# Other PSUM banks for the down projection, and the last two output products in halves of 160 columns

## The chip, the cores and the metric

The kernel runs on one core of a Trainium2 chip. The metric is the device time of one execution in microseconds; the median of three runs of the kernel before is 878.79 us (878.28 to 879.32). Beside the timed runs there is one profiled execution, from which all durations of instructions come.

## The reference, cut to what matters

```python
xn = layernorm(x)                                   # x: 2048 rows of 640, bf16
s  = attention(xn, k_cache, v_cache, wq, wo)         # 32 heads of 192, the last 512 keys
h  = silu(xn @ w_gate) * (xn @ w_up)                 # 2048 x 1536
g  = silu(h @ w_down)                                # 2048 x 640, the "down projection"
out = x + s * g                                      # s ends in the product with wo: 6144 -> 640
```

The change touches two products: `h @ w_down` and the last product with `wo`.

## The kernel before, in words

The kernel has three stages, one after the other on TensorE: the feed-forward part (to about 167 us), the attention (to about 690 us) and the output projection with the final multiply and add (to the end). The order of the work is written out by hand: each engine executes its instructions in the order in which the kernel emits them, and semaphore waits are put in by the framework from what each instruction reads and writes. For the PSUM tiles of the down projection these waits go by whole tile: an instruction that writes one half of a tile of two banks waits for an earlier reader of the other half.

**The feed-forward part.** Rows go in four blocks of 512 (`b` = 0 to 3). For each block twelve steps make gate and up products of 128 hidden columns (`ffn_hidden`, line 394: ten matmuls of 512 columns). Beside the steps of block `b` runs the down projection of block `b - 1`, so for the last block it runs alone, at the end of the stage (146 to 167 us). It is done by Strassen's scheme in Winograd's form, with seven products instead of eight for a 2 x 2 split: `ffn_down(b, u)` (line 442) takes a *row pair*, 128 rows and the 128 rows that stand 256 further on, `u` = 0 or 1, so two row pairs a block. It returns seven steps, which the caller issues in the order `w1, w2, w6, w5_, w7, w3, w4`, and `rest`. Each step is a product of six matmuls with 320 columns (line 456), and then reads by other engines:

- `w1`: product into bank U; ScalarE copies U to `p1` (line 478); for all but one row pair the sums S1 and S2 on VectorE follow here, for the first row pair of the last block they are made earlier (line 515).
- `w2`: product into bank V; VectorE makes `p1` = V + `p1` (line 484, in the helper at line 462).
- `w6`: adds a product with S2 to U; ScalarE copies U to `u2` (line 488) and applies the gate to `p1`; VectorE makes S3.
- `w5_`: product into bank W; ScalarE copies W to `w5` (line 494); VectorE makes S4.
- `w7`: adds a product with S3 to U; VectorE makes `w5` = U + `w5`.
- `w3`: adds a product with S4 to W; VectorE makes `u2` = W + `u2`; ScalarE gates `w5`.
- `w4`: adds a product to U; ScalarE gates U; the result is stored on SP's queue.

The banks are four halves of two PSUM tiles, `down_banks[0:4]`: 0 and 1 are the two banks of the first tile, 2 and 3 of the second. The kernel before takes three in rotation, from `3 * (2 * b + u)` on, modulo 4:

```
row pair        before (U, V, W)        tiles of U, V, W
b even, u = 0   0, 1, 2                 1st, 1st, 2nd
b even, u = 1   3, 0, 1                 2nd, 1st, 1st
b odd,  u = 0   2, 3, 0                 2nd, 2nd, 1st
b odd,  u = 1   1, 2, 3                 1st, 2nd, 2nd
```

For block 3, the last, the steps are issued one after the other; between them stand only products of the attention's first queries (`q_full`, line 523, five matmuls of 512 columns): for `u` = 0 one ahead of `w1`, one after `w5_` and one after `w4`; for `u` = 1 one after `w2`, one after `w5_` and one after `w4`. VectorE also makes combinations of `xc` (line 543) after `w2`, `w5_` and `w3`.

**The output projection.** Eight pairs of row tiles (`n` = 0 to 7), each again by seven products `M1, M7, M2, M5, M6, M4, M3` (`run`, `product`, line 942: 24 matmuls of 320 columns each, each with its own weight load). Each of the accumulators is a PSUM bank of its own, from a pool of eight. M3 adds to the bank that M5 began. After the last product, M3 of `n` = 7, the kernel has already multiplied and added all else (`u`), so two VectorE operations of 320 columns remain (line 979 in the helper `total`: the product times g, plus `u`), then the store of these 320 columns on ScalarE's queue.

Of the kernel before, what the change touches and what calls it, by code (L numbers as in the profile page):

```python
# [10 lines left out]
ALU = mybir.AluOpType  # L11
# [4 lines left out]
def kernel(  # L16
# [13 lines left out]
    nc = tc.nc  # L30
# [9 lines left out]
    W = min(4096, max(256, Sk // 4))  # L40
# [11 lines left out]
    HC = D // 2  # L52
# [27 lines left out]
    def sc_tile():  # L80
        return sc_pool.tile([P, 2, 512], f32, name="sc")

    def mm_tile(which=None):
        which = mm_next[0] if which is None else which
        mm_next[0] = 1 - which
        return mm_pool[0].tile([P, 2, 512], f32, name="mm", tag="mm%d" % which)
# [12 lines left out]
    M1, M7, M2, M5, M6, M4, M3 = PRODUCTS = range(10, 17)  # L99
# [127 lines left out]
    a_q, b_w = {}, {}  # L227

    with ExitStack() as fctx:
# [45 lines left out]
        for t in range(4, 8):  # L275
# [9 lines left out]
        first = [  # L285
            [gu[:, s, :] for s in range(2)]
            for gu in (sc_tile(), sc_tile(), psum1.tile([P, 2, 512], f32, name="gu"))
        ]
# [143 lines left out]
        down_banks = []  # L432
# [9 lines left out]
        def ffn_down(b, u):  # L442

            if not down_banks:
                down_banks.extend(t[:, n, 0:HC] for t in (mm_tile(), mm_tile()) for n in range(2))
            at = 3 * (2 * b + u)
            U, V, W = (down_banks[(at + k) % 4] for k in range(3))
            g = {}

            def a(side, k):  # L450
                rows = slice((u + 2 * side) * P, (u + 2 * side + 1) * P)
                return hTs[b][:, k * KD : (k + 1) * KD, rows]

            def mm(m, left, ps, first=True):
                for c in range(KD):
                    nc.tensor.matmul(  # L456
                        ps, left[:, c, :], D_OF[m][:, c, :],
                        start=(first and c == 0), stop=(c == KD - 1), skip_group_check=True,
                    )

            def total(to, x, y, op=ALU.add):
                nc.vector.tensor_tensor(to, x, y, op)

            def gate(side, n, x):
                nc.scalar.activation(g[side][:, n * HC : (n + 1) * HC], x, ACT.Silu)

            def store(side):
                nc.sync.dma_start(out=g_d[4 * b + u + 2 * side, :, :], in_=g[side][:])

            def sums():  # L470
                total(S1, a(1, 0), a(1, 1))
                total(S2, S1, a(0, 0), ALU.subtract)

            def w1():
                for side in range(2):
                    g[side] = ffa.tile([P, D], bf, name="g_t", bufs=2)
                mm(W1, a(0, 0), U)
                nc.scalar.copy(p1, U)
                if (b, u) != (NB - 1, 0):
                    sums()  # L480

            def w2():
                mm(W2, a(0, 1), V)
                total(p1, V, p1)

            def w6():
                mm(W6, S2, U, False)
                nc.scalar.copy(u2, U)
                gate(0, 0, p1)
                total(S3, a(0, 0), a(1, 0), ALU.subtract)  # L490

            def w5_():
                mm(W5, S1, W)
                nc.scalar.copy(w5, W)
                total(S4, a(0, 1), S2, ALU.subtract)

            def w7():
                mm(W7, S3, U, False)
                total(w5, U, w5)

            def w3():
                mm(W3, S4, W, False)
                total(u2, W, u2)
                gate(1, 1, w5)

            def w4():
                mm(W4, a(1, 1), U, False)
                gate(1, 0, U)
                store(1)

            def rest():
                gate(0, 1, u2)
                store(0)

            if (b, u) == (NB - 1, 0):
                sums()
            return [w1, w2, w6, w5_, w7, w3, w4], rest
# [93 lines left out]
        for b in range(NB):  # L611
# [3 lines left out]
            for f in range(NF):  # L615
# [15 lines left out]
                at = (b - 1) * NF + f  # L631
# [302 lines left out]

        nc.vector.tensor_tensor(a_s[n, m][:], part(x), part(y), op)

    def product(n, m, ps, first=True, ns=1):
        at = a_s[n, m] if (n, m) in a_s else a_q[n, A_OF[m][0]]
        w = HC // ns
        for k in range(ns):  # L940
            for c in range(KH):
                nc.tensor.matmul(  # L942
                    ps[k] if ns > 1 else ps, at[:, c, :], b_w[m][:, c, k * w : (k + 1) * w],
                    start=(first and c == 0), stop=(c == KH - 1), skip_group_check=True,
                )

    def load_xg(n):
        for side, r in enumerate(ROW_PAIRS[n]):
            tag, bufs = ("khat", 2) if n % 2 == 0 else (("K_p", "KT")[side], 1)
            t = xg[n, side] = kpool.tile([P, 2, D], bf, name="xg", tag=tag, bufs=bufs)  # L950
            nc.sync.dma_start(out=t[:, 0, :], in_=x2[r * P : (r + 1) * P, :])
            nc.sync.dma_start(out=t[:, 1, :], in_=g_d[r, :, :])
# [3 lines left out]
    def f_tile(n, k):  # L956
        return temps[:, 4 * (n % 2) + k, :]

    def finish(n, side, k, s, in_psum=False):

        t, cols = xg[n, side], slice(k * HC, (k + 1) * HC)
        y = f_tile(n, 3) if in_psum else s
        nc.vector.tensor_tensor(y, s, t[:, 1, cols], ALU.mult)
        nc.vector.tensor_tensor(t[:, 0, cols], y, t[:, 0, cols], ALU.add)

    def store(n, side, cols=slice(0, D), eng=nc.sync):
        r = ROW_PAIRS[n][side]
        eng.dma_start(out=out2[r * P : (r + 1) * P, cols], in_=xg[n, side][:, 0, cols])

    V = nc.vector  # L970

    ORDER = [(n, m) for ms in ((M1, M7), (M2,), (M5,), (M6,), (M4,), (M3,)) for n in range(2) for m in ms]
# [3 lines left out]
    acc = {}  # L976

    def total(to, x, y, op=ALU.add):
        V.tensor_tensor(to, x, y, op)

    def bank(n, name):
        acc[n, name] = late[1].tile([P, 512], f32, name="acc")[:, 0:HC]
        return acc[n, name]

    def run(n, m):

        ahead = n + 2 < len(ROW_PAIRS)
        u, v, c = (f_tile(n, k) for k in range(3))
        if m == M1:
            ps = bank(n, "M1+M2")  # L990
            product(n, M1, ps)
            nc.scalar.copy(u, ps)  # L992
        elif m == M7:
            ps = bank(n, "M7+M4")
            product(n, M7, ps)
            nc.scalar.copy(v, ps)
        elif m == M2:
            ps = acc[n, "M1+M2"]
            product(n, M2, ps, first=False)
            finish(n, 0, 0, ps, in_psum=True)  # L1000
            if (n, M3) == ORDER[-1]:
                store(n, 0, slice(0, HC))
        elif m == M5:
            ps = bank(n, "M5+M3")
            product(n, M5, ps)
            total(v, ps, v)
        elif m == M6:
            ps = bank(n, "M6")
            product(n, M6, ps)
            total(u, ps, u)  # L1010
            total(v, u, v)
            finish(n, 1, 1, v)
            for q in (A11, A21) if ahead else ():
                load_a(n + 2, q)
        elif m == M4:
            ps = acc[n, "M7+M4"]
            product(n, M4, ps, first=False)
            total(c, ps, u)
            finish(n, 1, 0, c)
            store(n, 1)  # L1020
            if ahead:
                load_a(n + 2, A22)
        else:
            ps, t, last_cols = acc[n, "M5+M3"], xg[n, 0], slice(HC, D)
            if (n, m) == ORDER[-1]:
                total(u, u, t[:, 1, last_cols], ALU.mult)
                total(u, u, t[:, 0, last_cols])
            product(n, M3, ps, first=False)
            if (n, m) == ORDER[-1]:
                total(c, ps, t[:, 1, last_cols], ALU.mult)  # L1030
                total(t[:, 0, last_cols], c, u)
                store(n, 0, last_cols, nc.scalar)
            else:
                total(u, ps, u)
                finish(n, 0, 1, u)
                store(n, 0)
            if ahead:
                load_a(n + 2, A12)
                load_xg(n + 2)
        if (n, m) in A_SUMS:  # L1040
            k = A_SUMS.index((n, m)) + 3
            if k < len(A_SUMS):
                a_sum(*A_SUMS[k])
# [46 lines left out]
    for n in range(4):  # L1090
        part = (n * KH // 4, (n + 1) * KH // 4)
# [80 lines left out]
    for n, m in ORDER:  # L1172
        run(n, m)
# [30 lines left out]
```

## Time and profile before

| | us |
|---|---|
| median of three runs | 878.79 |
| profiled execution | 878.91 |
| its span, first to last instruction | 877.1 |
| TensorE busy | 867.6 |
| VectorE busy | 603.5 |
| ScalarE busy | 427.5 |
| GpSimd busy | 114.2 |

The mean granted TensorE clock is 1.000. The 1.8 us between the span and the time of the profiled execution lie outside what the profile shows. In lines of the trace in order of time, the first number is the start in us from the span's start, the second the length of the group in us, then engine, line, operation, output and inputs, shapes and count; in brackets stands how long the engine had been idle just before, and what ended that. "PE" is TensorE's matmuls, "PEld" its weight loads, "SPq" and "ACTq" are the instructions that issue transfers. A matmul's duration (0.299 us for 320 columns) is longer than the distance to the next one's start (0.136 us), since matmuls are pipelined.

### The profile page before, as it was taken

The page shows a single profiled execution, that of the slowest core. Times are in us where ns is not written, and L with a number is a line of the kernel's source. Part 1 is how long each engine was busy: PE and PEld are TensorE (multiplying, and loading weights), DVE is VectorE, ACT ScalarE, POOL GpSimd, SP SyncE. Part 2 cuts the span into 40 slices and gives each one's busy share as a digit, 9 for nine tenths or more (in the row PEclk, how much of TensorE's full clock was granted, in tenths as well). Part 3 has the DMA queues.
Part 4 walks back from the last instruction along what each step waited for, and adds up shares of the span by engine and source line. Part 5 has one row for each costly group of instructions (what it writes and reads, how often), then busy time and mean ns, then how long its engine had stood idle before and what let it go on. Part 6 is the DMA issues. An engine that isn't in the chain of part 4 may idle for free.

```text
span 877.1 us, 22922 instructions
## 1 busy us (share of the span) xinstructions
PE 867.6 (99%) x9641; PEld 576.2 (66%) x9657; DVE 603.5 (69%) x1028; ACT 427.5 (49%) x649; POOL 114.2 (13%) x217
## 2 busy tenths in 40 slices
PE   8999999999999999999999999999999999999998
PEld 5455555567667667667667667667667777777775
DVE  6765876676876876876876876877775556555553
ACT  4264433665765765765765765765767300000000
POOL 0000000112122122122122132132120000000000
PEclk9999999999999999999999999999999999999999
DMA  9669974258999988977987777978899998645510
GB/s 294 172 210 275 214 222 116 67 98 180 204 204 217 201 179 200 195 162 176 198 177 179 176 149 163 208 165 189 167 230 251 255 355 294 212 171 176 176 54 16
DMA packets 273432, 165.52 MB, mean 189 GB/s; under 512 B 174384, under 2 KB 268208, under 8 KB 272816
## 3 DMA queue, kind: packets, MB, share of 16 engines
q1 hardware_dynamic: 271824, 156.08, 73.8%
q10 hardware_dynamic: 1504, 7.96, 2.6%
q8 instruction: 76, 1.25, 0.6%
q14 instruction: 28, 0.23, 0.1%
HBM read 89.95 MB, written 40.24 MB: 148 GB/s over the span
## 4 chain that ended last, share of the span: by engine, by line
PE 96%; DMA 1%; SPq 1%; DVE 1%; issue 0%; ACT 0%; ACTq 0%; DVEq 0%
PE acc L942 19%; PE sc L785 18%; PE mm L731 13%; PE sc L394 11%; PE mm L824 10%; PE sc L824 9%; PE mm L717 8%; PE mm L456 5%; PE sc L523 1%; DMA OT_b<-O_last 1%; DMA wg_sb<-in_B_w_gate_dram 1%; PE gu L394 0%; SPq L921 0%; DVE wq_p L174 0%; SPq L859 0%
## 5 line engine op out<-in xcount | busy, mean ns | idle before, releaser
L789 ACT ACTIVATE p_t<-sc 128x1024 bf16<-128x1024 f32 x256 | 253.6, 1024 | 59.8 <-PE sc L785 55.2
L785 PE MATMUL sc<-qT,khat 64*128 64x512 bf16 x1536 | 198.1, 376 | 0.0
L824 PEld LDWEIGHTS <-p_t 64*128 64x128 bf16 x4096 | 173.0, 94 | 8.6
L785 PEld LDWEIGHTS <-khat 64*128 64x128 bf16 x1536 | 89.0, 94 | 75.2 <-issue 0.5
L824 PE MATMUL mm<-V_p,p_t 64*128 64x193 bf16 x2112 | 111.6, 243 | 0.0
L824 PE MATMUL sc<-V_p,p_t 64*128 64x193 bf16 x1984 | 104.8, 243 | 0.0
L731 PE MATMUL mm<-xc,wq_p 64*128 64x512 f16 x750 | 94.4, 376 | 0.0
L942 PEld LDWEIGHTS <-a_s 128*128 128x128 f16 x768 | 75.1, 98 | 29.2
L731 PEld LDWEIGHTS <-wq_p 64*128 64x128 f16 (+1 forms) x1050 | 58.4, 94 | 47.9
L722 DVE TENSOR_REDUCE qT<-mm 128x512 bf16<-128x1024 f32 x66 | 80.6, 1222 | 13.0 <-PE mm L717 10.5
L769 POOL TENSOR_TENSOR m_f<-m_f 128x1024 f32<-128x1024 f32 x28 | 65.8, 2349 | 178.3 <-DVE qT L764 178.3
L853 ACT ACTIVATE O_b<-sc,r 128x192 bf16<-128x192 f32 x120 | 43.9, 419 | 86.7 <-PE sc L824 83.9
L717 PE MATMUL mm<-xnT,wq_p 64*128 64x512 bf16 x660 | 83.0, 376 | 0.5 <-DVE qT L722 0.4
L942 PE MATMUL acc<-b_w,a_q 128*128 128x320 bf16 (+1 forms) x576 | 81.8, 299 | 0.2 <-ACT xc L992 0.2
L942 PE MATMUL acc<-b_w,a_s 128*128 128x320 f16 (+1 forms) x576 | 81.8, 299 | 0.0
L992 ACT COPY xc<-acc 128x320 f32<-128x320 f32 x8 | 3.4, 428 | 141.5 <-PE acc L942 130.8
L942 PEld LDWEIGHTS <-a_q 128*128 128x128 bf16 x576 | 56.3, 98 | 22.3 <-issue 0.5
L394 PE MATMUL sc<-xnT,wg_sb 128*128 128x512 bf16 (+1 forms) x247 | 59.5, 353 | 2.1 <-DMA wg_sb<-in_B_w_gate_dram 1.1
L717 PEld LDWEIGHTS <-wq_p 64*128 64x128 bf16 x660 | 36.4, 94 | 36.8 <-issue 5.6
L401 ACT ACTIVATE sg<-sc 128x512 bf16<-128x512 f32 x46 | 27.3, 595 | 68.1 <-PE sc L394 66.3
L394 PE MATMUL sc<-xnT,wu_sb 128*128 128x512 bf16 (+1 forms) x260 | 60.3, 355 | 0.0
L764 DVE TENSOR_TENSOR qT<-mm,m_f 128x1024 bf16<-128x1024 f32 x30 | 36.7, 1224 | 31.9 <-ACT m_f L761 31.9
(110 smaller groups left out, 906.2 us busy)
## 6 DMA issues: line engine op xcount, KB each, us to landing
o_d<-OT_b SPq DMA_DIRECT2D x64, 384.0 KB, 5.6
a_q<-o_d SPq DMA_DIRECT2D x28, 768.0 KB, 5.9
won<-in_A_wo_dram SPq DMA_DIRECT2D x24, 320.0 KB, 4.2
wo_d<-wo_s SPq DMA_DIRECT2D x24, 320.0 KB, 2.7
wq_rows<-in_A_wq_dram SPq DMA_DIRECT2D x16, 480.0 KB, 4.8
wq_rows<-in_A_wq_dram SPq DMA_DIRECT2D x30, 240.0 KB, 5.8
K_p<-in_A_k_cache_dram SPq DMA_DIRECT2D x32, 192.0 KB, 5.8
V_p<-in_A_v_cache_dram SPq DMA_DIRECT2D x32, 192.0 KB, 3.2
```

The lines of the kernel that those rows point to most:

```text
L394: nc.tensor.matmul(out, w_sb[:, c, f * P : (f + 1) * P], xnT[:, c, qc], start=(c == 0), stop=(c == NC - 1),)
L456: nc.tensor.matmul(ps, left[:, c, :], D_OF[m][:, c, :], start=(first and c == 0), stop=(c == KD - 1), skip_group_check=True,)
L717: nc.tensor.matmul(q_ps[:, h, :], w[r, AS_IS[j], c, :], xnT[r, c, b * 512 : (b + 1) * 512], start=(c == 0), stop=(c == NC - 1),)
L722: nc.vector.reduce_sum(q_of(i, j), q_ps[:, :, :].rearrange("p h n -> p n h"), axis=AX.X)
L731: nc.tensor.matmul(ps[:, h, :], ws[h][r, c, :], xs[h][r, c, :], start=(first and c == 0), stop=(c == NC - 1), skip_group_check=True,)
L764: nc.vector.tensor_tensor(q_pair(i)[:, 1:4:2, :], st["ps"][:, :, :], m_f[:, SIDE_S, ::-1, :], ALU.add)
L769: eng.tensor_tensor(m_f[:, SIDE_S, :, :], diag, m_f[:, SIDE_S, :, :], ALU.subtract)
L785: nc.tensor.matmul(sc[:, h, :], khat[r, j, ks], q_of(i, j)[r, :], start=(j == 0), stop=(j == 2))
L789: nc.scalar.activation(p_t[:, :, :], sc[:, :, :], ACT.Exp, scale=scale)
L824: m = nc.tensor.matmul(acc[:, k, h * 256 : h * 256 + Dh + 1], Ps[i][kc][r, h, qt * P : (qt + 1) * P], V_p[r, kc, h, 0 : Dh + 1], start=(p ...
L853: nc.scalar.activation(O_b[:, qt, h, :], a_k[:, h, 0:Dh], ACT.Copy, scale=r[:, k, h, :])
L942: nc.tensor.matmul(ps[k] if ns > 1 else ps, at[:, c, :], b_w[m][:, c, k * w : (k + 1) * w], start=(first and c == 0), stop=(c == KH - 1), ...
```

## The change

There are two edits.

1. `ffn_down` no longer rotates the banks. U, V, W are banks 0, 2, 3 for `u` = 0 and 1, 3, 2 for `u` = 1, in every block: U always in the first PSUM tile, V and W in the second.
2. `product` can take a list of banks; it then makes the product in as many column slices, one after the other, each with all 24 contraction steps. For `n` = 7 M5 and M3 get two banks of 160 columns each, in place of one of 320. After M5 VectorE adds each half to `v` by itself. After M3 each half gets its multiply, its add and its store; the first half's store goes on SP's queue, the second's on ScalarE's. All other products stay in one bank.

```diff
-            at = 3 * (2 * b + u)
-            U, V, W = (down_banks[(at + k) % 4] for k in range(3))
+            U, V, W = (down_banks[k] for k in ((0, 2, 3), (1, 3, 2))[u])
...
-    def product(n, m, ps, first=True, ns=1):
+    def product(n, m, ps, first=True):
         at = a_s[n, m] if (n, m) in a_s else a_q[n, A_OF[m][0]]
-        w = HC // ns
-        for k in range(ns):
+        pss = ps if isinstance(ps, list) else [ps]
+        w = HC // len(pss)
+        for k, ps in enumerate(pss):
             for c in range(KH):
                 nc.tensor.matmul(
-                    ps[k] if ns > 1 else ps, at[:, c, :], b_w[m][:, c, k * w : (k + 1) * w],
+                    ps[:, 0:w], at[:, c, :], b_w[m][:, c, k * w : (k + 1) * w],
                     start=(first and c == 0), stop=(c == KH - 1), skip_group_check=True,
                 )
...
         elif m == M5:
-            ps = bank(n, "M5+M3")
-            product(n, M5, ps)
-            total(v, ps, v)
+            pss = [bank(n, "M5+M3"), bank(n, "M5+M3'")] if (n, M3) == ORDER[-1] else [bank(n, "M5+M3")]
+            product(n, M5, pss)
+            w = HC // len(pss)
+            for k, ps in enumerate(pss):
+                total(v[:, k * w : (k + 1) * w], ps[:, 0:w], v[:, k * w : (k + 1) * w])
...
-            product(n, M3, ps, first=False)
-            if (n, m) == ORDER[-1]:
-                total(c, ps, t[:, 1, last_cols], ALU.mult)
-                total(t[:, 0, last_cols], c, u)
-                store(n, 0, last_cols, nc.scalar)
+                pss = [ps, acc[n, "M5+M3'"]]
+                product(n, M3, pss, first=False)
+                w = HC // len(pss)
+                for k, ps in enumerate(pss):
+                    part, cols = slice(k * w, (k + 1) * w), slice(HC + k * w, HC + (k + 1) * w)
+                    total(c[:, part], ps[:, 0:w], t[:, 1, cols], ALU.mult)
+                    total(t[:, 0, cols], c[:, part], u[:, part])
+                    store(n, 0, cols, (nc.sync, nc.scalar)[k])
             else:
+                product(n, M3, ps, first=False)
```

## The prediction

> **What bounds the kernel now.** I read the page first (busy shares and the chain that ended last), then the busy time of TensorE in a few stretches, then the lines that the change touches.
>
> ```profile
> PE 867.6 (99%) x9641; PEld 576.2 (66%) x9657; DVE 603.5 (69%) x1028; ACT 427.5 (49%) x649; POOL 114.2 (13%) x217
> PE 96%; DMA 1%; SPq 1%; DVE 1%; issue 0%; ACT 0%; ACTq 0%; DVEq 0%
> ```
>
> TensorE carries 96% of the chain. The stretches say how closely:
>
> ```profile
> 148.00:152.00 4.00, 2.78 (x19) 1.72 (x18) 1.60 (x3) 1.12 (x3) 0.00 (x0) 1.00 0.24 82
> 175.00:700.00 525.00, 524.86 (x7343) 358.69 (x7340) 381.18 (x652) 341.70 (x470) 106.88 (x198) 1.00 0.87 188
> 704.00:874.00 170.00, 169.53 (x1248) 121.86 (x1246) 97.23 (x132) 5.89 (x15) 0.00 (x0) 1.00 0.53 184
> ```
>
> The second column is the length of the stretch, the third TensorE's busy time. Over the 525 us of attention it is idle 0.14 us, over the 170 us of the output projection about 0.5 us; between 148 and 152 us it is idle 1.22 us. A microsecond taken out of TensorE's queue therefore shows at the end, and there is one place with a microsecond to take. The down projection's line names it:
>
> ```profile
> its engine sat idle before it (us, times) until:
>   issue: 1.6, 2
>   DVE qT L462: 0.7, 1
>   ACT qT L478: 0.6, 1
> ```
>
> ("issue" is the queue of weight loads in the same two places.) In order of time:
>
> ```profile
> 148.19 0.98 PE L456 MATMUL mm<-wd_sb,hT 128*128 128x320 bf16 x6
> 149.26 0.43 ACT L478 COPY qT<-mm 128x320 f32<-128x320 f32 x1 [0.28 <-PE mm L456]
> 149.74 0.98 PE L456 MATMUL mm<-wd_sb,hT 128*128 128x320 bf16 x6 [0.57 <-ACT qT L478]
> 150.82 0.49 DVE L462 TENSOR_TENSOR qT<-mm,qT 128x320 f32<-128x320 f32 x1 [2.37 <-PE mm L456]
> 151.37 0.97 PE L456 MATMUL mm<-wq_p,khat 128*128 128x320 f16 x6 [0.65 <-DVE qT L462]
> ```
>
> These are `w1`, the copy of its bank U into p1, `w2` into bank V, the sum p1 = V + p1, and `w6`, for the last 512 rows' first row pair. U and V are here the two halves of one PSUM tile: `w2` waits for the copy out of U although it writes V, and `w6` for the sum that reads V although it writes U. The other place is the end:
>
> ```profile
> 870.11 3.42 PE L942 MATMUL acc<-b_w,a_s 128*128 128x320 bf16 x24
> 871.77 1.01 DVE L979 TENSOR_TENSOR xc<-xc,xg 128x320 f32<-128x320 f32 x2
> 873.57 0.49 DVE L979 TENSOR_TENSOR xc<-acc,xg 128x320 f32<-128x320 f32 x1 [0.79 <-PE acc L942]
> 874.09 0.49 DVE L979 TENSOR_TENSOR xg<-xc 128x320 bf16<-128x320 f32 x1
> 874.62 0.34 ACTq L968 DMA_DIRECT2D out_dram<-xg  x1
> ```
>
> After the last matmul come two VectorE operations of 320 columns, a store, and its landing.
>
> **Part 1: the banks.** In the changed kernel U lies in the first PSUM tile for every row pair, V and W in the second. I lay out 148 to 152 us again. One product of six matmuls is six starts at 0.136 us (0.815 us until the next can start). `w1` starts its last matmul at 148.87, so `w2` may start at 149.01 instead of 149.74. It now waits only for the previous pair's last sum out of the second tile, which VectorE ended at 147.40 (146.92 + 0.48). `w6` may follow at 149.82; it writes U and still needs the copy out of U, which ends at 149.69 and releases TensorE 0.05 later (as at 149.69 to 149.74 now): 149.74, in time. Its left operand S2 is ready from 148.46. `w5` could start at 150.64. It writes W, which now shares a tile with V, so it is the new holder of the wait for p1 = V + p1: `w2` ends at 149.99, VectorE starts 0.11 later (150.72 to 150.82 now), takes 0.49, and releases 0.05 after: 150.64. That is a tie, so I count no stall, with 0.1 us as its doubt. Before, `w5` started at 152.18. Gain: 152.18 - 150.64 = 1.54 us. It is more than the 1.22 us of idle time, because the last matmul's run-out (0.16 us) of both products is hidden again.
>
> What is late next? Behind `w5`, VectorE has a combination of xc (0.69), S3 (0.56), S4 (0.55, needed by `w3` 2.71 us after `w5` starts), and an xc of 0.95; counted from `w5`'s start they end 0.67, 1.26, 1.73 and 2.71 us after it, and the sum after `w7` starts at 2.98. ScalarE has the copies of u2 and W. All are as they stood, or earlier, against `w5`. The second row pair's `w1` newly shares a tile with the first pair's U and waits for its gate: that ended at 157.16, `w1` started at 157.60, so 0.44 us of cover remain. In the loop over the earlier blocks one product stands beside ten matmuls of 512 columns (2.16 us); a typical gate there is 54.04 to 54.48 and the next `w1` at 56.00. Those waits were covered on the old banks and are on the new ones: nothing gained, nothing lost. Stores of g and loads for the first pair are released by this same work and move with it, on SP's queue too.
>
> **Part 2: the last M5 and M3 in two banks of 160 columns.** 48 matmuls of 320 columns become 96 of 160, each with its own weight load, 48 loads more. The trace has no 160. Its starts stand 215.8, 135.8 and 55.7 ns apart for 512, 320 and 128 columns, a line of 0.4167 ns a column plus 2.4 ns: 69.1 ns for 160. The 128 columns bound it from below:
>
> ```profile
> 14.23 0.44 PE L394 MATMUL sc<-xnT,wg_sb 128*128 128x128 bf16 x5
> 14.51 0.44 PE L394 MATMUL sc<-xnT,wu_sb 128*128 128x128 bf16 x5
> ```
>
> Five matmuls, each with a weight load of 0.098 us, every 0.28 us. From above: 98 ns, if those loads did not overlap. I take 69.1, since it is nearest the 128-column rows. Cost: 24 x (2 x 69.1 - 135.8) = 0.06 us for M5, and 0.06 for M3's end (start of the last matmul 0.125 later, the matmul itself 0.067 shorter): +0.12 us.
>
> Here a rule speaks against the change. The Trainium skill, TensorE: Matmul & The Clock Gate, section Back-to-back issue gap, puts a stream of weight load and matmul pairs at about 81 ns each for 128 columns; the rows above show 55.7 and disagree. By the rule 96 x 81 - 48 x 135.8 = +1.26 us in place of +0.12.
>
> M5's sum becomes two VectorE operations; VectorE idles 2.3 us before it and 2.7 us after, so nothing. At the end the first half's two operations run under the second half's matmuls: VectorE is free of the two older operations at 872.84 (872.78 + 0.06), the first half's last about 873.56, and the second half's product ends at 873.65. What remains on the path are two operations of 160. Rows: 0.49 at 320, 0.69 at 512, so 1.04 ns a column: 0.32 each (between 0.25, half, and 0.49). Gain 2 x 0.167 = 0.33 us. No VectorE instruction of the second half waits for the first half's store in the built program's list of waits, and the ScalarE store waits for two loads long done.
>
> The last store shrinks to 40 KB:
>
> ```profile
> out_dram<-xg SPq DMA_DIRECT2D x1, 160.0 KB, 1.8
> out_dram<-xg ACTq DMA_DIRECT2D x1, 80.0 KB, 1.6
> ```
>
> The next halving gives some 0.1 us, between 0 and 0.2. SP's closing list of waits has the last store's semaphore last instead of last but one, 0.06 us (876.24 to 876.30). Together 0.15. The added store's issue on SP (0.34 us) starts at about 873.6 on an otherwise empty queue and lands before the last one.
>
> **Sum.** -1.54 + 0.12 - 0.33 - 0.15 = -1.90 us. The profiled execution took 878.91 (span 877.1 and 1.8 around it), giving 877.01; the median of the runs is 878.79, 0.12 lower: 876.9.
>
> **The rivals.**
> 1. The weight loads set the pace of the halved products, one every 98 ns (their mean at line 942), each beside a matmul but not beside another load: 96 x 98 - 6.52 = +2.89 us in place of +0.12, in all +0.87: 879.7, no change that can be told. For it: the left operands of M5 and M3 are f16, and no row shows full f16 loads closer than 136 ns. Against: bf16 loads of the same 98 ns start 55.7 ns apart. By the page's 81 ns this rival would end at 878.0.
> 2. Slower: a weight load in the halved products overlaps not even the matmul before it: 98 + 69 = 167 ns a pair, 96 x 167 - 6.52 = +9.5 us, 886.3. It decides from 89 ns on (96 x 89 - 6.52 = 2.02, all that the rest gains). Against: weight loads and matmuls overlap in every row.
> 3. The stall of part 1 only moves: `w5` waits, because VectorE takes the xc combination (0.69 us) before the sum: -1.21, 877.6. Against: the program's order has the sum first, and VectorE idles 2.37 us there.
> 4. Part 1's gain is eaten on entering attention, where VectorE holds TensorE for 0.37 us at 174.82: 878.4. Against: that VectorE burst starts from TensorE's own product at 169.63.
>
> **How the numbers follow.** A measurement of this kernel tells about 0.2%, 1.76 us: 877.03 and 880.55 are the bounds. My forecast has 0.72, and its own doubts (0.1 at `w5`, 0.1 at the landing, some 0.4 between runs, which spread over 1.0) put about two thirds of it below 877.03. Rival 1: 0.07; 2: 0.04; 3: 0.08; 4: 0.04; a larger gain, near 876.3, from transfers that land earlier around 700 us: 0.05. Faster 0.72 x 0.67 + 0.05 = 0.53, slower 0.04, the rest within. The range, 876.2 to 878.2, takes in rival 3 and the larger gain, and leaves out rivals 1, 2 and 4, 0.15.
>
> **What will show it.** Right: no wait named at line 455 between 148 and 152 us, `w5` 1.5 us earlier; matmuls of 160 columns 69 ns apart; VectorE's last two at 0.32; the last issue about 1.75 us earlier. Wrong: a wait for VectorE ahead of `w5`, starts 80 ns or more apart in the last product, or TensorE idle between 166 and 704 us by more than the 0.7 us of now.

## The result, and the profile after

The changed kernel takes 877.25 us (median of 22 runs, 876.28 to 879.32) against 878.67 us before (22 runs, 877.80 to 879.84). The ratio is 0.9985, 95% interval 0.9978 to 0.9991: about 1.3 us faster, between 0.8 and 1.9 us. The profiled execution has a span of 874.5 us against 877.1; it was the fastest of the 22 runs, and the 2.6 us between the two spans are more than the change gives, as the stretches below show.

The stall of the down projection is gone. The same list for its line, now 455, is empty:

```profile
its engine sat idle before it (us, times) until:
who waited for it (us, times):
```

TensorE's matmuls and the two reads that it used to wait for, in order of time in the changed kernel:

```profile
147.73 1.79 PE L455 MATMUL mm<-wd_sb,hT 128*128 128x320 bf16 x12
148.80 0.42 ACT L477 COPY qT<-mm 128x320 f32<-128x320 f32 x1 [0.28 <-PE mm L455]
149.36 0.98 PE L455 MATMUL mm<-wq_p,khat 128*128 128x320 f16 x6
149.63 0.49 DVE L461 TENSOR_TENSOR qT<-mm,qT 128x320 f32<-128x320 f32 x1 [1.63 <-PE mm L455]
150.17 0.98 PE L455 MATMUL mm<-m_f,wq_p 128*128 128x320 f16 x6
```

`w1` and `w2` are now one row of twelve matmuls, `w6` follows at 149.36 and `w5` at 150.17. `w5` starts 2.44 us after `w1`, where it took 3.99 us before. VectorE's sum ends at 150.12, 0.05 us ahead of `w5`: the tie that was reckoned.

The end:

```profile
867.91 3.48 PE L942 MATMUL acc<-b_w,a_s 128*128 128x160 bf16 x48
869.57 1.01 DVE L979 TENSOR_TENSOR xc<-xc,xg 128x320 f32<-128x320 f32 x2
870.50 0.32 DVE L979 TENSOR_TENSOR xc<-acc,xg 128x160 f32<-128x160 f32 x1
870.85 0.33 DVE L979 TENSOR_TENSOR xg<-xc 128x160 bf16<-128x160 f32 x1
871.43 0.33 DVE L979 TENSOR_TENSOR xc<-acc,xg 128x160 f32<-128x160 f32 x1 [0.25 <-PE acc L942]
871.79 0.32 DVE L979 TENSOR_TENSOR xg<-xc 128x160 bf16<-128x160 f32 x1
872.14 0.34 ACTq L968 DMA_DIRECT2D out_dram<-xg  x1
```

The first half's operations lie under the second half's matmuls. After the product two operations of 0.32 to 0.33 us remain. The transfers out, by size and median time to landing:

```profile
out_dram<-xg SPq DMA_DIRECT2D x1, 160.0 KB, 1.8
out_dram<-xg SPq DMA_DIRECT2D x1, 40.0 KB, 1.5
out_dram<-xg ACTq DMA_DIRECT2D x1, 40.0 KB, 1.5
```

Where the 2.6 us between the two spans lie is best seen from five stretches, each the distance between two matmuls' starts in a trace (the first begins and the last ends with the span). The kernels of the experiments are in the table too, and are explained below; "chip 1" and so on tell only which of them ran on one chip together.

| us | to the first down product | to the last down matmul | to the first output product | to the last matmul of the last M4 | to the end | span |
|---|---|---|---|---|---|---|
| before | 37.34 | 127.98 | 525.15 | 179.49 | 7.15 | 877.12 |
| changed | 36.88 | 126.44 | 525.03 | 179.42 | 6.73 | 874.50 |
| changed, chip 3 | 37.56 | 126.44 | 525.01 | 179.25 | 6.72 | 874.99 |
| banks alone, chip 1 | 39.05 | 126.44 | 525.01 | 180.18 | 7.14 | 877.83 |
| banks alone, chip 3 | 36.44 | 126.44 | 525.02 | 179.17 | 7.15 | 874.22 |
| halves alone, chip 1 | 38.48 | 127.98 | 525.15 | 179.76 | 6.72 | 878.09 |
| halves alone, chip 3 | 36.66 | 127.98 | 525.14 | 179.23 | 6.72 | 875.74 |

In these seven profiles the second, third and last columns repeat to 0.02 us and move with the parts of the change: -1.54, -0.13 and -0.43 us. The fourth holds the halved M5, +0.06 (179.17 to 179.23, both on chip 3 and without a wait). That is -2.04 us for the change. The rest of the 2.6 us is in the first column and in a wait inside the fourth, which differ between profiles of one and the same kernel: 36.44 to 39.05 us for the start, where TensorE waits for the first loads, and up to 0.85 us of waiting near 703 us.

### The profile page after: what moved, and what is told of

It is laid out like the page before. It is cut to its first block, busy times and chain, and to the rows that moved or that the text cites. A ratio compares the mean times of both kernels' runs of the same rounds, so it can differ in the third digit from the quotient of the medians.

```text
span 874.5 us, 23024 instructions
## 1 busy us (share of the span) xinstructions
PE 868.0 (99%) x9689; PEld 578.3 (66%) x9705; DVE 604.0 (69%) x1031; ACT 427.4 (49%) x649; POOL 114.1 (13%) x217
## 4 chain that ended last, share of the span: by engine, by line
PE 98%; DVE 1%; DMA 1%; issue 0%; ACT 0%; ACTq 0%
PE acc L942 21%; PE sc L784 19%; PE mm L730 13%; PE sc L394 11%; PE mm L823 10%; PE sc L823 10%; PE mm L716 8%; PE mm L455 5%; PE sc L522 1%; DMA x_t<-in_A_x_dram 1%; PE gu L394 0%; DVE wq_p L174 0%; DVE qT L721 0%; ACTq L250 0%; DVE wd_sb L440 0%
## 5 line engine op out<-in xcount | busy, mean ns | idle before, releaser
L942 PEld LDWEIGHTS <-a_s 128*128 128x128 f16 x816 | 77.1, 98 | 27.4
L942 PE MATMUL acc<-b_w,a_s 128*128 128x320 f16 (+2 forms) x600 | 81.9, 294 | 0.0
```

The source lines that it names most:

```text
L942: nc.tensor.matmul(ps[:, 0:w], at[:, c, :], b_w[m][:, c, k * w : (k + 1) * w], start=(first and c == 0), stop=(c == KH - 1), skip_group_ch ...
```

## The experiments

The theory, A: each part's gain in the trace reaches the end whole, and the distance between the medians (1.4 us) and the traces' sum is the spread of the runs. Two rivals: B, part of what the banks give is taken back later; C, the tail's gain is lost in the landing.

**One part alone.** The banks alone: the kernel before with

```diff
-            at = 3 * (2 * b + u)
-            U, V, W = (down_banks[(at + k) % 4] for k in range(3))
+            U, V, W = (down_banks[k] for k in ((0, 2, 3), (1, 3, 2))[u])
```

> The new banks alone, the last two products as before. Theory A (each part's gain in the trace reaches the end whole, and the medians' 1.42 us is short of the traces' sum by the spread of the runs): no idle time at line 455, w5 1.54 us earlier against w1 than before, and a time 1.5 us (0.17%) below the kernel before. Theory B (part of what the banks give is taken back between 167 and 870 us): the same 1.54 us up to w5, but from w5 to the start of the last M3 some 0.4 us more than before, and a time only about 1.1 us below. Theory C (the tail's gain is lost in the landing, the banks give all): 1.4 to 1.5 us below, and the halves alone give nothing.

Measured: 877.54 us against 879.02 before on the same chip, ratio 0.9984 (0.9975 to 0.9993). TensorE does not idle at the down projection's line; the stretch from there to the first output product is 525.01 us, shorter than before, not longer. The longer fourth stretch (180.18) is the wait near 703 us, which this profile shows at its longest:

```profile
703.72 0.33 ACTq L901 DMA_DIRECT2D b_w<-wo_d  x1
704.09 0.43 ACT L991 COPY xc<-acc 128x320 f32<-128x320 f32 x1 [11.43 <-PE acc L941]
704.57 1.65 PE L941 MATMUL acc<-b_w,a_q 128*128 128x320 bf16 x11 [0.85 <-ACT xc L991]
```

The halves alone: the changed kernel with the rotation put back.

```diff
-            U, V, W = (down_banks[k] for k in ((0, 2, 3), (1, 3, 2))[u])
+            at = 3 * (2 * b + u)
+            U, V, W = (down_banks[(at + k) % 4] for k in range(3))
```

> The halves of 160 columns alone, the banks in rotation as before. Theory A: the stall of 0.57 and 0.65 us is back at the same two products, and from the start of the last M3 to the span's end the stretch is 0.40 us shorter than before (6.99 to about 6.59 us), the time 0.3 to 0.4 us (0.04%) below the kernel before, hardly to be told. Theory C: the stretch from the last M3 to the end of the span is as before, 6.9 to 7.0 us, and so is the time.

Measured: 878.82 us against 879.02, ratio 0.9998 (0.9989 to 1.0006). The stall is back, with the idle times of the kernel before, and the last stretch is 6.72 us, 0.43 us shorter. C does not hold in the trace; the time alone could not tell 0.4 us from nothing.

**Which tiles are shared.** Two other ways to pair the three banks in two tiles. U with V, for both row pairs:

```diff
-            U, V, W = (down_banks[k] for k in ((0, 2, 3), (1, 3, 2))[u])
+            U, V, W = (down_banks[k] for k in ((0, 1, 2), (2, 3, 0))[u])
```

> As the changed kernel, but U and V are always the two banks of one tile, for both row pairs (0, 1, 2 and 2, 3, 0). If sharing a tile is the cause of the stall, and cover by other products decides what it costs: in the last block the first row pair stalls as in the kernel before (1.54 us against the changed kernel), the second stalls ahead of w2 (0.73 us) but not ahead of w6, which has a product of 1.08 us before it; in the loop, with 2.16 us of other products between steps, nothing. In all 2.3 us (0.26%) above the changed kernel, 0.4 us above the kernel before. If it is something else in the rotation (the order of banks from block to block), the second row pair shows no wait and the time is that of the kernel before less 0.4.

Measured: 879.49 us against 879.02, ratio 1.0004 (0.9995 to 1.0013). The matmuls of the last block, in order of time:

```profile
150.01 0.98 PE L455 MATMUL mm<-wd_sb,hT 128*128 128x320 bf16 x6 [0.57 <-ACT qT L477]
151.64 0.97 PE L455 MATMUL mm<-wq_p,khat 128*128 128x320 f16 x6 [0.65 <-DVE qT L461]
...
159.42 0.97 PE L455 MATMUL mm<-wd_sb,hT 128*128 128x320 bf16 x6 [0.57 <-ACT qT L477]
160.23 1.03 PE L522 MATMUL sc<-xnT,wq_p 128*128 128x512 bf16 x4
```

The second row pair stalls ahead of `w2` as well, and not ahead of `w6`, for which `q_full` (160.23) is the cover. At this line nothing waits in the loop. The stretch of the down projection is 128.98 us, 2.54 us longer than in the changed kernel; 0.27 us of that is a wait for a transfer of xnT at 110 us (0.11 idle and 0.16 of run-out), which leaves 2.27 for the 2.3 expected. Sharing decides which read is waited for, and cover decides whether it costs.

U with W:

```diff
-            U, V, W = (down_banks[k] for k in ((0, 2, 3), (1, 3, 2))[u])
+            U, V, W = (down_banks[k] for k in ((0, 2, 1), (1, 3, 0))[u])
```

> As the changed kernel, but W shares the tile with U and V stands alone (0, 2, 1 and 1, 3, 0). If a wait goes by tile and costs what is not covered, this third way to pair the banks costs most: w5 waits for the copy of U into u2 (0.75 us), w3 for the sum that reads U after w7 (0.81), w4 for the sum that reads W after w3 (0.81). In the last block 2.4 us for each row pair; in the loop only w4 follows w3 without other products between, 0.81 us for each of six row pairs. In all 4.7 + 4.9 = 9.6 us above the changed kernel. If tiles do not decide, the time is that of the changed kernel.

Measured: 888.67 us (the median of two runs) against 879.09 before on the same chip, ratio 1.0113 (1.0094 to 1.0131). The stretch of the down projection is 138.07 us, 11.63 us longer than in the changed kernel, where 9.6 were expected. What was mis-sized is the wait in the loop:

```profile
51.61 0.98 PE L455 MATMUL mm<-wd_sb,qT 128*128 128x320 bf16 x6
53.58 0.97 PE L455 MATMUL mm<-m_f,hT 128*128 128x320 f16 x6 [0.99 <-DVE qT L461]
```

```profile
52.44 0.69 DVE L402 TENSOR_TENSOR hT<-sc,sg 128x512 bf16<-128x512 f32 x1 [1.89 <-ACT sg L401]
53.05 0.48 DVE L461 TENSOR_TENSOR qT<-mm,qT 128x320 f32<-128x320 f32 x1
```

The sum that `w4` waits for stands behind the multiply of the hidden block on VectorE, so TensorE idles 0.99 us and not 0.65 in five of the six row pairs of the loop, and 1.13 us in the sixth. With the run-out of the product before it (0.16 us) that is 7.06 us in all where 4.86 were expected. The two row pairs of the last block cost 4.58 us where 4.74 were expected. The two differences, 2.20 and -0.16, make up the 2.0 us.

**The pace of weight loads.** M5 and M3 of the last row tiles in four banks of 80 columns:

```diff
-            pss = [bank(n, "M5+M3"), bank(n, "M5+M3'")] if (n, M3) == ORDER[-1] else [bank(n, "M5+M3")]
+            pss = [bank(n, "M5+M3" + "'" * k) for k in range(4 if (n, M3) == ORDER[-1] else 1)]
...
-                pss = [ps, acc[n, "M5+M3'"]]
+                pss = [acc[n, "M5+M3" + "'" * k] for k in range(4)]
...
-                    store(n, 0, cols, (nc.sync, nc.scalar)[k])
+                    store(n, 0, cols, (nc.sync, nc.scalar)[k % 2])
```

> As the changed kernel, but M5 and M3 of the last row tiles in four banks of 80 columns, 96 matmuls and weight loads a product. It measures the pace of pairs of weight load and matmul for f16 weights. If the columns alone set the distance: 35.7 ns, product 3.4 us. If the loads have a floor as the 128 columns of the feed-forward part show: about 56 ns, 5.35 us a product, the time about 3.9 us above the changed kernel (2 x 2.03, less 0.16 for two shorter operations at the end). By the skill's 81 ns: 7.8 us a product, 8.8 us above. If loads do not overlap each other: 98 ns, 9.4 us a product, 12 us above.

Measured: 877.70 us against 879.02, ratio 0.9986 (0.9977 to 0.9995). The changed kernel did not run on this chip, so quarters and halves are compared by their traces. M5 in the profile, with the product after it:

```profile
858.94 3.60 PE L942 MATMUL acc<-xc,a_s 128*128 128x80 f16 x96
862.38 0.85 PE L942 MATMUL acc<-b_w,a_s 128*128 128x320 f16 x5
```

96 pairs of a full f16 weight load and a matmul take 862.38 - 858.94 = 3.44 us, 35.8 ns each: the line through 512, 320 and 128 columns gives 35.7. So loads set no floor here down to 80 columns, and rivals 1 and 2 of the prediction fall. The tail itself is longer than with halves: from the last matmul of the last M4 to the end it takes 7.39 us in this profile, and 6.72 to 6.73 with halves. M3 takes 0.15 of that. The eight operations of 0.23 to 0.24 us now follow one another on VectorE without a wait, so VectorE and not the last slice sets the last store, which is issued 1.01 us after the last matmul's start (0.99 with halves). From that issue to the end it is 0.49 us longer. The four stores of 20 KB land 2.55, 2.29, 2.04 and 1.78 us after their issue, in their order.

That does not show that small stores are slow. The store of 160 KB ahead of them landed after 3.7 us, in place of 1.8: its last eight packets of 128 moved only from 873.06 on, when a transfer of 16 KB of instructions, begun at 871.43, had run to its end at 873.07. The last packets of the four small stores moved after those eight. In all other profiles the last such transfer is over at least 6.4 us before the end. One profile cannot tell whether it falls there in every run of this kernel.

**How tight the tie is.** The sum p1 = V + p1 in two operations:

```diff
-                total(p1, V, p1)
+                for k in range(2):
+                    part = slice(k * HC // 2, (k + 1) * HC // 2)
+                    total(p1[:, part], V[:, part], p1[:, part])
```

> As the changed kernel, but the sum p1 = V + p1 is made in two operations of 160 columns, 0.2 us longer together (2 x 0.33 + 0.03 against 0.49). If the tie at w5 in the last block is as tight as reckoned, w5 there waits for VectorE by 0.2 us, and nowhere else (the second row pair has a product of 1.08 us between w2 and w6, the loop 2.16 us): 0.2 us above the changed kernel. If there is slack, no wait is seen.

Measured: 876.40 us against 879.09, ratio 0.9973 (0.9963 to 0.9983).

```profile
149.26 0.98 PE L455 MATMUL mm<-wq_p,khat 128*128 128x320 f16 x6
149.53 0.56 DVE L461 TENSOR_TENSOR qT<-mm,qT 128x160 f32<-128x160 f32 x2 [1.63 <-PE mm L455]
150.14 0.57 PE L455 MATMUL mm<-m_f,wq_p 128*128 128x320 f16 x3
```

The two operations, of which neither reads what the other writes, overlap: they took 0.56 us together and not 0.69. So VectorE's sum was made 0.07 us longer, not 0.2, and `w5` is late by as much: 150.14, where 149.26 + 0.815 = 150.08. The tie is real, but the time cannot show 0.07 us. The ratio, lower than the changed kernel's first one, raised the question whether the chip or the variant made it.

**The wait near 703 us.** M4's weights loaded on SP's queue instead of ScalarE's:

```diff
-    load_b(M4, late[0])
+    load_b(M4, late[0], nc.sync)
```

> As the changed kernel, but the load of M4's weights for the output projection is issued on SP's queue and not on ScalarE's. In the profiles taken so far TensorE stands idle between 0 and 0.85 us near 701 to 705 us (0.16 before, none in the changed kernel, 0.85, 0.36, 0.36 and 0.80 in the four variants), always until ScalarE's first copy of M1, which stands behind the issue of this load, which waits for a transpose to land. Theory A says that this, with the transfers at the start and near 36 us, is where runs differ by more than the parts of the change: then the idle time is gone in every run, the copies come some 10 us earlier, and the time falls by 0.3 to 0.5 us (0.05%) against the changed kernel, 1.8 us (0.2%) against the kernel before. If the idle time has another cause, the copy moves but the wait stays, and the time is that of the changed kernel, 1.4 us below the one before.

Measured: 876.54 us against 879.09, ratio 0.9970 (0.9960 to 0.9981). ScalarE's first copies of M1 come at 692.24, as soon as the product is done, and TensorE no longer waits there:

```profile
692.24 0.42 ACT L992 COPY xc<-acc 128x320 f32<-128x320 f32 x1 [1.32 <-PE acc L942]
695.50 0.42 ACT L996 COPY xc<-acc 128x320 f32<-128x320 f32 x1 [2.83 <-PE acc L942]
```

That the copy stood behind the transfer's issue is shown. Whether it costs time on average needed the changed kernel beside it.

**All together on one chip.** The changed kernel, the variant with M4 on SP's queue, the banks alone and the halves alone, with the kernel before at 878.73 us.

> The changed kernel itself, beside the other three on one chip, since the kernels compared so far ran on two chips: on the second chip two variants of the changed kernel stood 2.6 us below the kernel before, where the changed kernel's own result is 1.4 us. If the two parts reach the end whole, 1.9 us (0.22%) below the kernel before. If one of the two variants had removed a loss that the changed kernel has, it stays near 1.4 us here too, and 1 us above the variant with M4's load on SP.

> The changed kernel with M4's weights loaded on SP's queue, beside the changed kernel on the same chip. If the wait for ScalarE's first copy near 703 us is what it removes: the mean idle time there in the profiles, 0.3 to 0.5 us, below the changed kernel, with no idle time there in its profile. If the earlier 2.6 us was the chip: the same time as the changed kernel within 0.2 us.

> The banks alone, on the same chip as the changed kernel: 1.5 us (0.17%) below the kernel before, 0.36 us above the changed kernel, by the stretches of the trace.

> The halves alone, on the same chip as the changed kernel: 0.36 us (0.04%) below the kernel before, 1.5 us above the changed kernel, by the stretches of the trace.

| on chip 3 | median us | ratio to before | 95% interval | gain expected, us | by the medians, us |
|---|---|---|---|---|---|
| changed | 876.44 | 0.9973 | 0.9962 to 0.9984 | 1.9 | 2.3 |
| M4's load on SP | 876.55 | 0.9975 | 0.9965 to 0.9984 | 2.2 to 2.4, or as changed | 2.2 |
| banks alone | 877.44 | 0.9985 | 0.9976 to 0.9994 | 1.5 | 1.3 |
| halves alone | 878.27 | 0.9999 | 0.9991 to 1.0008 | 0.36 | 0.5 |

The changed kernel stands at 0.9973 here, so the lower ratios of the two variants were not theirs. The two parts add up to 1.8 us by the medians, which these intervals do not tell from the 2.3 of both together. The load on SP's queue gives nothing that shows, and this chip could not tell what it is worth: the changed kernel's own profile has no wait near 703 us here either. That wait was 0.16 and 0.03 us in the first profiles of the kernel before and the changed one, 0.36 to 0.85 us in the four profiles on chip 1, 0.32 us in one on the second chip, and 0 in all on chip 3. No version is shown to beat the changed kernel.

## Why the prediction was right, and where not

**What bounds the kernel** held: apart from the start and the wait near 703 us, no stretch that the change does not touch is longer than before, so a microsecond out of TensorE's queue is a microsecond off the span. B falls by this: from the last down product to the first output product the kernels without rotation take 525.00 to 525.03 us, before 525.15. The one exception is the variant with the sum in two, with 525.31 us and a wait of 0.13 us of its own near 431 us.

**Part 1** was right in place, cause and size: `w2` and `w6` in a row, the wait handed to `w5` and met there in a tie, 1.54 us forecast and 1.54 us in the stretch. One sentence of it reads its rows wrongly: VectorE's work behind `w5` is not "as it stood, or earlier" against `w5`. The combination of xc ended 0.14 us ahead of `w5` before (152.04 against 152.18) and ends 0.67 us behind it now (150.84 against 150.17). This costs nothing, as the ends that the prediction gives there imply: S4 is done at 151.88, and `w3`, which needs it, starts at 152.88. That nothing would be gained or lost in the loop held as well, and the two other pairings show why: what waits there is either covered by 2.16 us of other products or, as with `w4` behind `w3`, not covered at all.

**Part 2** was right term by term: 69.2 ns a pair (M5's 48 in 3.32 us) for 69.1; the last matmul 0.126 us later in M3 for 0.125; the path from the last matmul's start to the last issue 1.39 to 0.99 us, for 0.33 of VectorE and 0.07 of a shorter last matmul; from there to the span's end 2.51 to 2.36 us for the 0.15 forecast. The row of 128 columns was the right one to go by, and the rivals of serial loads fall. The 81 ns for 128 columns of the Trainium skill (TensorE: Matmul & The Clock Gate, section Back-to-back issue gap) is not met here: the pairs stand 55.7 ns apart at 128 columns and 69.2 at 160.

**What it did not have**: 0.13 us in the attention. In all three profiles with rotating banks one row of twelve score matmuls takes 1.46 us from start to start, and 1.29 in the others. This is that row in the chain that ended last, in the kernel before (first line) and in the changed one:

```profile
392.82 1.46 PE sc L785 x12
390.81 1.29 PE sc L784 x12
```

Of these 0.17 us some 0.04 are made up in the next two rows. The three profiles also show TensorE waiting 0.14 us for ScalarE's copy at line 761 near 470 us, but that is not the difference: the others wait as long, once, for ScalarE's `p_t` (near 624 us in the changed kernel), and either wait delays the matmuls behind it by 0.28 us. Why the banks of the feed-forward part should decide about the 0.17 us was not tried, and stays open.

**The sum** of 1.90 us stands against 2.04 us in the traces (1.91 without the 0.13 that it did not have), and against 1.3 us (0.8 to 1.9) in the first comparison and 2.4 us (1.4 to 3.3, ratio 0.9973) on chip 3. The median forecast, 876.9 us, was 0.35 us below the measured 877.25 and inside the range. The chance given to a gain of over 0.2%, 0.53, was a toss between two outcomes that this kernel's runs hardly tell apart: the first comparison came out at 0.15%, the second at 0.27%. That the first one is smaller than the traces' sum is not explained by the change: what differs between profiles is the start (2.6 us between the shortest and the longest) and the wait near 703 us (0 to 0.85 us), and both are as large as what is sought. That these made the difference in those 22 runs was argued and not shown.

## What to carry to other kernels

Where a framework's waits go by whole PSUM tile, choose which banks share a tile by who reads them next: pair those whose reader is done, or whose next writer has other work in front. With three banks in two tiles, the three pairings cost 0, 2.3 and 11.6 us here. When a wait is moved, compute at whom it arrives and with what slack, and read the gain from the stretch of the trace that it is in, because a change of 0.2% may be at the edge of what the times tell.

## What the runs showed of the hardware that was not expected

A stream of full 128 x 128 f16 weight loads, each with a matmul of 80 columns, runs at 35.8 ns a pair although each load is recorded as about 100 ns: nearly three recorded loads overlap. Two VectorE operations of 160 columns without a dependency took 0.56 us together (they start 0.24 us apart and last 0.32 us each), and dependent ones of that size, in the tail, start 0.35 to 0.36 us apart. Where a transfer of 16 KB of instructions, 1.64 us long, ran beside a store of 160 KB, eight of the store's 128 packets moved only at its end, and the store landed 3.7 us after its issue in place of 1.8.
